# A spectral layer and two gated feed-forward layers: the first batch's inverse through memory, nine warming matmuls, shorter last stores

## The chip, the cores and the metric

The kernel runs on one NeuronCore of a Trainium2 chip. The metric is the device time of one execution in microseconds (us), the median of the runs shown.

## What is computed

`x` is 2 batches of 3008 rows by 256 columns, all in float32.

```python
X = np.fft.rfft(x, axis=1)                 # along the 3008 rows
Yr = Xr @ w_r - Xi @ w_i + b_r             # complex 256x256 mix
Yi = Xr @ w_i + Xi @ w_r + b_i
Y  = soft_threshold(Yr, 0.01) + 1j * soft_threshold(Yi, 0.01)
y  = np.fft.irfft(Y, n=3008, axis=1)       # 6016 rows by 256
y  = (sigmoid(y @ w_gate) * (y @ w_val)) @ w_out          # 256 -> 1536 -> 256
out = (silu(y @ w2_gate) * (y @ w2_val)) @ w2_out
```

## The kernel before, in words

**The transform.** 3008 is 47 times 64, and a row index splits into `(j, p)` with 94 values of `j` and 32 of `p`. A first transform over `j` is a matmul with a 94x96 table, a second one over the other index is a matmul with one 128x128 table for each of 24 frequency groups, two groups (`KP`) at a time. The inverse takes the same two steps backwards: 12 matmul steps with the table `i1c`, then 16 column pairs `c` with the table `f2s`. In between the data must change its layout.

**First batch** (`spectral_first`, L264 to L400, and `stage3` with `early` set). Its operands are plain float32, which TensorE takes in two passes; a profile counts each pass as one matmul. It starts with five matmuls on a zeroed bfloat16 tile (`warm`, L178 to L181, called at L299), whose result nobody reads. The first transform is L306: 9 tasks, 128 passes, with 94 rows of `x` as the stationary operand. It ends in SBUF (`zt`). For each of 12 steps `i` come four transposes (`turn`, L334), the second transform (`forward`, L242), the mix (L255, float32r operands, one pass each), the threshold and the inverse (L352). In the inverse the result `y` is stationary and the table moves, 128 columns at a time, so the result comes out with the channels on the partitions. ScalarE copies it into `zz` (L357), a tile that holds the whole batch. `stage3` then turns each column pair back by four transposes (L490), copies it to `z4` and multiplies by `f2s` (L501). The first `S3` = 6 pairs are done before the feed-forward loop begins (L636), the other 10 inside it, one for each unit.

**Second batch.** `spectral_second` does the same work inside the feed-forward loop, one piece per unit: `stage1` (16 column pairs, L219, three float32r matmuls each), `stage2` (12 steps) and `stage3`. Between its stages the data goes through two scratch tensors in memory, `scr1[1]` and `scr2[1]`: a store in one layout (L207, L454) and a load in the other (L408, L485). The first `E1` = 3 of its 16 column pairs are taken out of `stage1` and done ahead of the loop as one float32 matmul each (`fill`, L577); `filled` copies and stores them. Two of these matmuls stand beside the last inverse of the first batch, the third ahead of the loop.

**Feed-forward.** The rest, and most of the time, are units of 12 matmuls L636 and 6 matmuls L662 for each chunk of 512 rows and each of 12 weight blocks. VectorE and ScalarE decode the weights (`load_ff`) ahead of them.

**The end.** `turn_out` (L693 to L723) turns the last chunk of 384 rows and stores it to `out` by seven DMAs of 8, 94, 26, 68, 60, 34 and 94 rows of 1 KB, all on SP's queue.

**What sets the order.** Up to the feed-forward loop every engine follows the order in which the program is written. A DMA is issued by the engine that it is written for, in that engine's order: an SP instruction that waits holds what is behind it on SP.

Of the kernel before, what the change touches and what calls it, by code (L numbers as in the profile page):

```python
# [20 lines left out]
PP = 32  # L21
# [8 lines left out]
NA = 8  # L30
E1 = 3
S3 = 6
# [5 lines left out]
def tile_kernel(ctx, tc, x, w_r, w_i, b_r, b_i, wts, f1, f2, s2, i1, i1f, eye, one, out):  # L38
# [138 lines left out]

    def warm(n):  # L178
        for i in range(n):
            pw = ps_b.tile([P, 512], F32, tag="f", name=f"warm{i}")  # L180
            nc.tensor.matmul(pw, idle[:, 0:P], idle, start=True, stop=True)  # L181
# [81 lines left out]

    def spectral_first(zz, ps):  # L264
        NS = KH // KP
# [5 lines left out]
        with tc.tile_pool(name="z0", bufs=1, reuse_waits="tile") as z0:  # L271
# [8 lines left out]
            with tc.tile_pool(name="p1", bufs=1, reuse_waits="tile") as fp:  # L280
# [17 lines left out]
                nc.vector.memset(idle, 0.0)  # L298
                warm(5)  # L299
                next(tables)  # L300
# [26 lines left out]
            with tc.tile_pool(name="p2", bufs=1, reuse_waits="tile") as fp:  # L327
# [19 lines left out]
                def inverse(i, ks=range(KP)):  # L347
                    y, t = Y[i], table(i1c, i)
                    pi = bank(f"pi_0_{i}_{ks[0]}").rearrange("p (k d c) -> p k d c", k=KP, d=2)
                    for k in ks:  # L350
                        for d in range(2):
                            nc.tensor.matmul(pi[:, k, d, :], y[:, k, d * P:(d + 1) * P], t[:, k, :],  # L352
                                             start=True, stop=True)
                    k0, k1 = ks[0], ks[-1] + 1
                    dst = zz.rearrange("p d a (q k) -> p d (a q) k", q=4)
                    src = pi.rearrange("p k d c -> p d c k")
                    nc.scalar.copy(dst[:, :, :, KP * i + k0:KP * i + k1], src[:, :, :, k0:k1])  # L357

# [14 lines left out]
                for i in range(NS + 1):  # L373
                    if i + 1 < NS:
                        turn(i + 1)
                    if i < NS:
                        forward(i)
                    if i:
                        mix(i - 1, 0)
                    if 0 < i < last:  # L380
                        advance(dec, 1 + i % 2)
                    if i > last:
                        shrink(last, slice(0, 1))
                    if i > 1:
# [92 lines left out]

    def stage3(b, fp, ps, zz=None, direct=(), early=None):
        NS = PP // 2
        Z, V = {}, {}  # L480

        def load(c, ps):
            z4 = Z[c] = fp.tile([96, 2, 256], F32, tag="z4", bufs=4, name=f"z4_{b}_{c}")
            if zz is None:
                nc.sync.dma_start(z4, by_k1(scr2[b], slice(2 * c, 2 * c + 2)))  # L485
                return
            pt = ps.tile([P, 2, 256], F32, tag="f", name=f"p4_{b}_{c}")
            for q in range(2):
                for d in range(2):
                    nc.tensor.transpose(pt[:96, q, d * P:(d + 1) * P], zz[:, d, 2 * c + q, :], eyes)  # L490
            if early and c % 2:
                nc.vector.tensor_copy(z4, pt[:96])
            else:
                nc.scalar.copy(z4, pt[:96])

# [22 lines left out]

        c0 = 0
        if early:  # L520
# [9 lines left out]
        ps = ps[0] if early else ps  # L530
        ahead = 3 if zz is None else 1
        for c in range(c0 + len(Z), c0 + ahead):
            load(c, ps)
        for c in range(c0, NS):
            if c + ahead < NS:
                load(c + ahead, ps)
            inverse(c, ps)
            store(c)
            yield True

    def spectral_second(b, ps):
        with tc.tile_pool(name="fz", bufs=1, reuse_waits="tile") as fz:
            second = stage2(b, ps, fz)
            with tc.tile_pool(name="p1", bufs=1, reuse_waits="tile") as fp:
                for c, _ in enumerate(stage1(b, ps, fp, E1)):
                    if c == 5:
                        next(second)
                    yield True
# [3 lines left out]
        with tc.tile_pool(name="p3", bufs=2, reuse_waits="tile") as fp:  # L552
            yield from stage3(b, fp, ps)

# [7 lines left out]
    pz = pzs.enter_context(tc.tile_pool(name="pz", bufs=1, reuse_waits="tile", side="right"))  # L562
    zz = pz.tile([P, 2, PP, 96], F32, name="zz")
    f1f = pz.tile([NJ, P], F32, name="f1f")
# [4 lines left out]
    def load_fill(c):  # L569
        xb = x[1].rearrange("(j p) c -> j p c", p=PP)  # L570
        x1[c] = px.tile([NJ, 2, 256], F32, tag="x1", bufs=E1, name=f"x1_{c}")
        nc.sync.dma_start(x1[c][0:80], xb[0:80, 2 * c:2 * c + 2, :])
        nc.sync.dma_start(x1[c][80:94], xb[80:94, 2 * c:2 * c + 2, :])
# [5 lines left out]
    def filled(c, copy):  # L579
        z1 = px.tile([96, 2, 256], F32, tag="z1e", bufs=2, name=f"z1e_{c}")  # L580
        copy(z1, p1e.pop(c)[:96])
        nc.sync.dma_start(by_k1(scr1[1], slice(2 * c, 2 * c + 2)), z1)

    xs, late_ps = {}, []
    with tc.tile_pool(name="ps_b", bufs=8, space=PSUM) as ps_b:
        spectral_first(zz, ps_b)
        late_pools.append(ctx.enter_context(tc.tile_pool(name="wq", bufs=1, reuse_waits="tile")))
# [6 lines left out]
        def third_first():  # L594
            with tc.tile_pool(name="p3z", bufs=2, reuse_waits="tile") as fp:
                yield from stage3(0, fp, late_ps, zz, [split_x(0, c) for c in range(RC)], ps_b)
# [95 lines left out]
    def turn_out(ci, o):  # L692
# [9 lines left out]
        dst = out.rearrange("(b j p) c -> b p j c", b=B, p=PP)  # L702
        ob = mp.tile([P, 4, 256], F32, tag="ob", bufs=RC, name=f"ob{ci}")
        for j in range(0, tn, 256):
            pt = ps_f.tile([P, 2, 256], F32, tag="f", name=f"pt{ci}_{j}")
# [5 lines left out]
            for a, k in enumerate(js):  # L711
# [154 lines left out]
```

## Time and profile before

| what | value |
|---|---|
| median of 3 runs | 1378.81 us (1378.71 to 1380.22) |
| the profiled execution's own time | 1378.57 us |
| its span | 1376.5 us |
| TensorE busy (PE) | 1362.9 us, 99% of the span |
| VectorE busy (DVE) | 731.4 us, 53% |
| ScalarE busy (ACT) | 538.3 us, 39% |
| DMA, mean over the span | 55 GB/s |
| last matmul to the end of the span | 1366.85 to 1376.5 us |

Times in the profile are in us from the start of the span. The profile's chain that ended last lies on PE for 97% of the span, so what counts is how long PE takes from one matmul to the next. Matmuls overlap in the records: the time that one occupies is the distance from its start to the next start, not its length. PEclk is the TensorE clock that the profile shows as granted, as a share of full speed; GB/s is what the DMA engines moved.

### The profile page before, as it was taken

The numbers are of one execution on the slowest core, as the hardware profiler recorded it, in microseconds if no ns is written. First come the engines' busy times: TensorE is split into PE (matmuls) and PEld (weight loads), VectorE is DVE, ScalarE is ACT, GpSimd is POOL, SyncE is SP. The second block draws the span as 40 slices with busy tenths as digits, with TensorE's granted clock in tenths as the row PEclk, the third lists the DMA queues.
The fourth block names the chain that finished last, engine by engine and source line by source line (L and its number), as shares of the span: only waits on it lengthen the run. The fifth ranks groups of instructions, "written<-read, shape, count | busy, mean of one in ns | idle before, by whom it ended". The sixth has DMA issues, their size and how long they took to land.

```text
span 1376.5 us, 16890 instructions
## 1 busy us (share of the span) xinstructions
PE 1362.9 (99%) x6784; PEld 1163.2 (85%) x6784; DVE 731.4 (53%) x1110; ACT 538.3 (39%) x941; POOL 11.0 (1%) x26
## 2 busy tenths in 40 slices
PE   9999999999999999999999999999999999999997
PEld 8998888888888888888889988888888888888896
DVE  1558984555334865633344755555455555555553
ACT  1655554444334443433333433333333333333332
POOL 1000000000000000000000000000000000000000
PEclk9999999999999999999999999999999999999999
DMA  8222442333332320200002101001101101100000
GB/s 212 67 78 83 147 127 82 108 108 103 100 110 80 100 77 0 77 31 31 1 27 77 50 1 31 24 7 32 31 1 31 32 0 31 31 6 26 27 16 12
DMA packets 57202, 76.35 MB, mean 55 GB/s; under 512 B 6084, under 2 KB 40615, under 8 KB 57124
## 3 DMA queue, kind: packets, MB, share of 16 engines
q1 hardware_dynamic: 54980, 71.69, 17.0%
q0 software_dynamic: 2144, 3.58, 1.3%
q8 instruction: 53, 0.87, 0.3%
q14 instruction: 25, 0.20, 0.0%
HBM read 51.53 MB, written 23.72 MB: 55 GB/s over the span
## 4 chain that ended last, share of the span: by engine, by line
PE 97%; DMA 1%; DVE 1%; ACT 0%; SPq 0%; issue 0%; ACTq 0%
PE pg L636 56%; PE po L662 28%; PE pm L255 5%; PE p L501 2%; PE p L306 2%; PE p L242 1%; PE pi L352 1%; PE pt L710 1%; PE p L219 1%; PE pi L448 1%; PE p L490 1%; PE pt L334 0%; DMA xr<-in_x_dram 0%; DMA xin<-xT 0%; PE p1e L577 0%; DVE yl L440 0%
## 5 line engine op out<-in xcount | busy, mean ns | idle before, releaser
L636 PE MATMUL pg<-fxh,wh 128*128 128x512 f32 (+1 forms) x1152 | 446.1, 387 | 0.0
L636 PE MATMUL pg<-fxl,wh 128*128 128x512 f32 (+1 forms) x1152 | 443.5, 385 | 0.0
L636 PE MATMUL pg<-fxh,wl 128*128 128x512 f32 (+1 forms) x1152 | 443.4, 385 | 0.0
L640 ACT ACTIVATE sg<-pg 128x512 f32<-128x512 f32 (+1 forms) x288 | 169.6, 589 | 362.2 <-PE pg L636 361.6
L644 DVE TENSOR_TENSOR h<-sg,pg 128x512 f32<-128x512 f32 (+1 forms) x288 | 194.5, 675 | 188.8 <-ACT sg L640 183.7
L647 ACT CAST hh<-h 128x512 fp32r<-128x512 f32 (+1 forms) x288 | 176.6, 613 | 300.2 <-DVE h L644 299.2
L649 DVE TENSOR_TENSOR hl<-h,hh 128x512 fp32r<-128x512 f32 (+1 forms) x288 | 195.9, 680 | 154.7 <-ACT hh L647 152.3
L636 PEld LDWEIGHTS pg<-fxh,wl 128*128 128x128 f32 x1152 | 216.2, 188 | 41.4
L636 PEld LDWEIGHTS pg<-fxh,wh 128*128 128x128 f32 x1152 | 216.5, 188 | 41.0 <-DVE fxl L512 0.2
L636 PEld LDWEIGHTS pg<-fxl,wh 128*128 128x128 f32 x1152 | 216.4, 188 | 39.9 <-issue 0.2
L662 PE MATMUL po<-hh,wh 128*128 128x512 f32 (+1 forms) x576 | 223.6, 388 | 0.3 <-ACT hh L647 0.3
L662 PE MATMUL po<-hh,wl 128*128 128x512 f32 (+1 forms) x576 | 221.9, 385 | 0.0
L662 PE MATMUL po<-hl,wh 128*128 128x512 f32 (+1 forms) x576 | 221.6, 385 | 0.0
L642 DVE TENSOR_TENSOR sg<-sg,pg 128x512 f32<-128x512 f32 (+1 forms) x144 | 97.4, 676 | 157.9 <-ACT sg L640 157.7
L662 PEld LDWEIGHTS po<-hh,wl 128*128 128x128 f32 x576 | 108.1, 188 | 20.8
L662 PEld LDWEIGHTS po<-hh,wh 128*128 128x128 f32 x576 | 108.2, 188 | 20.5 <-ACT hh L647 0.6
L662 PEld LDWEIGHTS po<-hl,wh 128*128 128x128 f32 x576 | 108.2, 188 | 20.2 <-DVE hl L649 0.2
L255 PE MATMUL pm<-wmh,Xh 128*128 128x256 f32 x192 | 54.2, 282 | 0.9 <-DVE Xl L234 0.9
L255 PE MATMUL pm<-wmh,Xl 128*128 128x256 f32 x192 | 53.7, 280 | 0.0
L255 PE MATMUL pm<-wml,Xh 128*128 128x256 f32 x192 | 53.7, 280 | 0.0
L625 DVE TENSOR_TENSOR fxl<-xin,fxh 128x512 fp32r<-128x512 f32 (+1 forms) x44 | 28.5, 677 | 19.4 <-ACT fxh L624 19.2
L255 PEld LDWEIGHTS pm<-wmh,Xh 128*128 128x128 f32 x192 | 36.2, 188 | 3.1 <-DVE Xl L234 2.7
(103 smaller groups left out, 854.2 us busy)
## 6 DMA issues: line engine op xcount, KB each, us to landing
raw<-in_moe_w_gate_dram SPq DMA_DIRECT2D x24, 256.0 KB
raw<-in_moe_w_val_dram SPq DMA_DIRECT2D x24, 256.0 KB
raw<-in_moe_w_out_dram SPq DMA_DIRECT2D x24, 256.0 KB
xin<-x2T SPq DMA_DIRECT2D x11, 512.0 KB
xT<-xo SPq DMA_DIRECT2D x26, 188.0 KB
x2T<-xo SPq DMA_DIRECT2D x9, 512.0 KB
xin<-xT SPq DMA_DIRECT2D x8, 512.0 KB
i1s<-in_tab_i_dram POOLq DMA_DIRECT2D x12, 256.0 KB, 4.2
```

The costliest lines, as they stand in the source:

```text
L219: nc.tensor.matmul(pt[c][:96], f1s[:, w, :], v, start=(i == 0), stop=(i == 2))
L255: nc.tensor.matmul(pm[:, k, :], a, w, start=(j == 0), stop=(j == len(ops) - 1))
L306: nc.tensor.matmul(pt[:, a], xt[:, a, d * P:(d + 1) * P], f1f, start=True, stop=True)
L501: nc.tensor.matmul(pt[:, d, q * NJ:(q + 1) * NJ], z[:, q, d * P:(d + 1) * P], f2s, start=True, stop=True)
L625: nc.vector.tensor_tensor(xl[:, k, :tn], xin[:, k, :tn], xh[:, k, :tn], op=ALU.subtract)
L636: nc.tensor.matmul(pg[:, s, :tn], w[:, 2 * s + k, :], v[:, k, :tn], start=(i == 0), stop=(i == 5))
L640: nc.scalar.activation(sg[:, :tn], pg[:, 0, :tn], AF.Sigmoid)
L642: nc.vector.tensor_tensor(sg[:, :tn], sg[:, :tn], pg[:, 0, :tn], op=ALU.mult)
L644: nc.vector.tensor_tensor(h[:, :tn], sg[:, :tn], pg[:, 1, :tn], op=ALU.mult)
L647: nc.scalar.copy(hh[:, :tn], h[:, :tn])
L649: nc.vector.tensor_tensor(hl[:, :tn], h[:, :tn], hh[:, :tn], op=ALU.subtract)
L662: nc.tensor.matmul(o[d][:, :tn], w[:, 4 + d, :], v[:, :tn], start=(first and d not in [q for q, _, _ in ops[:i]]), stop=(last and d not in ...
```

## The change

The first batch's inverse now holds the table still and moves `y`, 256 columns at a time, so a result comes out in the layout that the second batch has. It is copied to a small tile `z3` and stored to `scr2[0]`; `stage3` loads it back in the other layout, seven column pairs (`Z4`) ahead. `zz` and the transposes L490 are gone. `E1` goes from 3 to 8: eight column pairs of the second batch are done as fills, seven of them between the last inverse and the first L501, with their copies on VectorE and ScalarE in turn and their stores on POOL's queue. `warm` runs nine matmuls in place of five. The last chunk's stores are cut to at most 80 rows; three of the now nine (34, 60 and 14 rows) are issued by ScalarE.

```diff
-E1 = 3
+E1 = 8
+Z4 = 7
...
-    def warm(n):
+    def warm(n, banks):
         for i in range(n):
-            pw = ps_b.tile([P, 512], F32, tag="f", name=f"warm{i}")
+            if i < banks:
+                pw = ps_b.tile([P, 512], F32, tag="f", name=f"warm{i}")
             nc.tensor.matmul(pw, idle[:, 0:P], idle, start=True, stop=True)
...
-                warm(5)
+                warm(9, 7)
...
                 def inverse(i, ks=range(KP)):
                     y, t = Y[i], table(i1c, i)
-                    pi = bank(f"pi_0_{i}_{ks[0]}").rearrange("p (k d c) -> p k d c", k=KP, d=2)
+                    k0, k1 = ks[0], ks[-1] + 1
+                    pi = bank(f"pi_0_{i}_{k0}").rearrange("p (k c) -> p k c", k=KP)
                     for k in ks:
-                        for d in range(2):
-                            nc.tensor.matmul(pi[:, k, d, :], y[:, k, d * P:(d + 1) * P], t[:, k, :],
-                                             start=True, stop=True)
-                    k0, k1 = ks[0], ks[-1] + 1
-                    dst = zz.rearrange("p d a (q k) -> p d (a q) k", q=4)
-                    src = pi.rearrange("p k d c -> p d c k")
-                    nc.scalar.copy(dst[:, :, :, KP * i + k0:KP * i + k1], src[:, :, :, k0:k1])
+                        nc.tensor.matmul(pi[:, k], t[:, k, :], y[:, k, :], start=True, stop=True)
+                    z3 = fp.tile([P, KP, 256], F32, tag="z3", bufs=2, name=f"z3_0_{i}_{k0}")
+                    nc.scalar.copy(z3[:, k0:k1], pi[:, k0:k1])
+                    nc.sync.dma_start(by_p(scr2[0], slice(KP * i + k0, KP * i + k1)), z3[:, k0:k1])
...
-                    if 7 < i < 8 + E1:
-                        load_fill(i - 8)
+                    if 1 < i < 2 + E1:
+                        load_fill(i - 2)
                 inverse(last, (0,))
                 fill(0)
                 inverse(last, (1,))
-                fill(1)
-                filled(0, nc.vector.tensor_copy)
-                filled(1, nc.vector.tensor_copy)
...
-        def load(c, ps):
-            z4 = Z[c] = fp.tile([96, 2, 256], F32, tag="z4", bufs=4, name=f"z4_{b}_{c}")
-            if zz is None:
-                nc.sync.dma_start(z4, by_k1(scr2[b], slice(2 * c, 2 * c + 2)))
-                return
-            pt = ps.tile([P, 2, 256], F32, tag="f", name=f"p4_{b}_{c}")
-            for q in range(2):
-                for d in range(2):
-                    nc.tensor.transpose(pt[:96, q, d * P:(d + 1) * P], zz[:, d, 2 * c + q, :], eyes)
...
+        def load(c):
+            Z[c] = zp.tile([96, 2, 256], F32, tag="z4", bufs=bufs, name=f"z4_{b}_{c}")
+            nc.sync.dma_start(Z[c], by_k1(scr2[b], slice(2 * c, 2 * c + 2)))
...
         if early:
-            for c in range(4):
-                load(c, early)
+            for c in range(bufs):
+                load(c)
+            yield True
             for c in range(S3):
                 inverse(c, early)
                 store(c)
-                if 4 + c <= S3:
-                    load(4 + c, early)
-            c0 = S3
+            c0, ahead = S3, bufs - 1
+            for c in range(bufs, c0 + ahead):
+                load(c)
...
     def filled(c, copy):
-        z1 = px.tile([96, 2, 256], F32, tag="z1e", bufs=2, name=f"z1e_{c}")
+        z1 = pz.tile([96, 2, 256], F32, tag="z1e", bufs=4, name=f"z1e_{c}")
         copy(z1, p1e.pop(c)[:96])
-        nc.sync.dma_start(by_k1(scr1[1], slice(2 * c, 2 * c + 2)), z1)
+        nc.gpsimd.dma_start(by_k1(scr1[1], slice(2 * c, 2 * c + 2)), z1)
...
         third = third_first()
         next(third)
-        fill(2)
-        filled(2, nc.vector.tensor_copy)
+        filled(0, nc.vector.tensor_copy)
+        for c in range(1, E1):
+            fill(c)
+            filled(c, nc.scalar.copy if c % 2 else nc.vector.tensor_copy)
+        next(third)
...
-                    step = min(n - r, NJ - jj)
-                    nc.sync.dma_start(dst[pcol // PP, pcol % PP, jj:jj + step, :], ob[r:r + step, k // 128, :])
+                    step = min(n - r, NJ - jj, 80 if end else NJ)
+                    late.append((dst[pcol // PP, pcol % PP, jj:jj + step, :], ob[r:r + step, k // 128, :]))
+                    if not end or k == 0 or step > 60:
+                        nc.sync.dma_start(*late.pop())
                     r += step
+            if j + 256 >= tn:
+                for pair in late:
+                    nc.scalar.dma_start(*pair)
```

**TensorE at the seam, before.** These are PE's instructions from the first batch's last inverse (`pi`) to its column pairs (`p`); `p1e` is a fill.

```order
L352 MATMUL pi_11_1_1026<-i1c_687,y_11_983 128x128 x2
L577 MATMUL p1e_1030<-x_1_872,f1f 128x512
L490 MATMUL p_0_0_1054<-eyes,zz 96x128 x4
L490 MATMUL p_0_1_1061<-eyes,zz 96x128 x4
L490 MATMUL p_0_2_1068<-eyes,zz 96x128 x4
L490 MATMUL p_0_3_1075<-eyes,zz 96x128 x4
L501 MATMUL p_0_0_1081<-f2s,z_0_0_1053 128x94 x4
L490 MATMUL p_0_4_1089<-eyes,zz 96x128 x4
L501 MATMUL p_0_1_1095<-f2s,z_0_1_1060 128x94 x4
```

The transposes read `zz` and stand ahead of each column pair.

The same place in the changed kernel, whose line numbers are its own (L354 is the inverse, L564 the fill, L488 the column pair):

```order
L354 MATMUL pi_11_1_1047<-y_11_1003,i1c_704 128x256
L564 MATMUL p1e_1084<-x_1_512,f1f 128x512
L564 MATMUL p1e_1089<-x_2_574,f1f 128x512
L564 MATMUL p1e_1094<-x_3_638,f1f 128x512
L564 MATMUL p1e_1099<-x_4_706,f1f 128x512
L564 MATMUL p1e_1104<-x_5_767,f1f 128x512
L564 MATMUL p1e_1109<-x_6_830,f1f 128x512
L564 MATMUL p1e_1114<-x_7_895,f1f 128x512
L488 MATMUL p_0_0_1119<-f2s,z_0_0_1067 128x94 x4
L488 MATMUL p_0_1_1126<-f2s,z_0_1_1069 128x94 x4
```

Seven fills now stand where the first transposes stood, and the column pairs follow one on another.

**SP's queue at the seam, changed.** `scr_0` is `scr2[0]`, `z_0_11_0` and `z_0_11_1` are the last two `z3` tiles, the other `z` are `z4` tiles. Before the change SP issued nothing for these.

```order
L357 DMA scr_0_78<-z_0_10_0_1022 128x512
L357 DMA scr_0_78<-z_0_11_0_1042 128x256
L357 DMA scr_0_78<-z_0_11_1_1049 128x256
L481 DMA z_0_0_1067<-scr_0_78 96x2x256
L481 DMA z_0_1_1069<-scr_0_78 96x2x256
L481 DMA z_0_2_1071<-scr_0_78 96x2x256
L481 DMA z_0_3_1073<-scr_0_78 96x2x256
L481 DMA z_0_4_1075<-scr_0_78 96x2x256
```

Every load of `z4` reads from all 12 stores, so the first one waits on SP until the last store has landed.

## Rows read from the trace of the kernel before

**Rows 1.** The page: the chain that ended last, by engine.

```profile
PE 97%; DMA 1%; DVE 1%; ACT 0%; SPq 0%; issue 0%; ACTq 0%
```

**Rows 2.** Timeline of PE, 0 to 45 us: start, length, instruction, passes, [idle before <-releaser].

```profile
1.19 2.31 PE L181 MATMUL warm<-idle 128*128 128x512 bf16 x5 [1.19 <-DVE idle L298]
4.22 3.75 PE L306 MATMUL p<-f1f,xr 94*128 94x128 f32 x16 [0.71 <-DMA f1f<-in_tab_f_dram]
8.28 24.23 PE L306 MATMUL p<-f1f,xr 94*128 94x128 f32 x112 [0.31 <-DMA xr<-in_x_dram]
32.31 0.42 PE L334 MATMUL pt<-eyes,zt 128*128 128x128 f32 x1
...
34.50 1.67 PE L242 MATMUL p<-s2c,z 128*128 128x128 f32 x8
36.01 0.60 PE L334 MATMUL pt<-eyes,zt 128*128 128x128 f32 x4
36.44 1.06 PE L242 MATMUL p<-s2c,z 128*128 128x128 f32 x8
37.26 0.36 PE L255 MATMUL pm<-bmov,ones 128*128 128x256 f32 x1
```

**Rows 3.** Windows of the start: length, busy time by engine, PEclk, DMA share, GB/s.

```profile
0.00:17.40 17.40, 15.18 (x64) 13.22 (x65) 2.10 (x5) 3.29 (x7) 4.47 (x14) 1.00 0.93 202
17.40:20.40 3.00, 3.00 (x16) 3.00 (x16) 0.56 (x1) 0.27 (x1) 0.00 (x0) 1.00 1.05 281
```

**Rows 4.** Windows, the stretch in which DVE makes the mix tables (same columns).

```profile
29.60:35.12 5.52, 5.33 (x25) 4.70 (x25) 2.95 (x8) 1.79 (x4) 0.00 (x0) 1.00 0.07 26
```

**Rows 5.** Timeline of PE, 97 to 110 us, the seam to the feed-forward loop.

```profile
97.50 1.02 PE L577 MATMUL p1e<-x,f1f 94*128 94x512 f32 x2
98.36 0.61 PE L352 MATMUL pi<-i1c,y 128*128 128x128 f32 x4
98.80 1.02 PE L577 MATMUL p1e<-x,f1f 94*128 94x512 f32 x2
99.85 1.95 PE L490 MATMUL p<-eyes,zz 128*96 128x128 f32 x16
...
102.51 0.60 PE L490 MATMUL p<-eyes,zz 128*96 128x128 f32 x4
102.95 1.03 PE L501 MATMUL p<-f2s,z 96*128 96x94 f32 x8
103.81 0.60 PE L490 MATMUL p<-eyes,zz 128*96 128x128 f32 x4
...
108.69 0.80 PE L636 MATMUL pg<-fxh,wh 128*128 128x512 f32 x1
```

**Rows 6.** Timeline of PE, 183 to 193 us: a column pair of the second batch's first stage.

```profile
186.98 0.63 PE L219 MATMUL p<-xh,f1s 94*96 94x512 f32 x2
...
187.68 0.40 PE L636 MATMUL pg<-fxh,wh 128*128 128x512 f32 x1
```

**Rows 7.** Timeline of all engines, 352 to 363 us: SP at the second batch's seam.

```profile
353.28 0.33 SPq L454 DMA_DIRECT2D scr<-z  x1
...
355.48 1.80 SPq L485 DMA_DIRECT2D z<-scr  x4
```

**Rows 8.** Windows, 356.5 to 359.8 us, while those four loads land.

```profile
356.50:359.80 3.30, 3.30 (x20) 2.78 (x19) 0.69 (x1) 0.74 (x2) 0.00 (x0) 1.00 0.73 233
```

**Rows 9.** Timeline, 1355 to 1377 us: the last matmuls and the last stores on SP.

```profile
1365.81 1.04 PE L710 MATMUL pt<-eyes,ot 128*128 128x128 f32 x6 [0.18 <-ACT ot L699]
...
1367.17 2.39 SPq L721 DMA_DIRECT2D out_dram<-ob  x7
```

**Rows 10.** Windows of the end, 1370.0 to 1375.5 us.

```profile
1370.00:1370.50 0.50, 0.00 (x0) 0.00 (x0) 0.00 (x0) 0.00 (x0) 0.00 (x0) 0.71 0.50 92
...
1371.50:1372.00 0.50, 0.00 (x0) 0.00 (x0) 0.00 (x0) 0.00 (x0) 0.00 (x0) 0.50 0.14 49
...
1375.00:1375.50 0.50, 0.00 (x0) 0.00 (x0) 0.00 (x0) 0.00 (x0) 0.00 (x0) 0.50 0.00 0
```

More of the change, by code (lines that the diff above doesn't have):

```diff
@@ L260, in shrink_of, with spectral_first @@
         nc.vector.scalar_tensor_tensor(out=y, in0=pm, scalar=LAM, in1=y, op0=ALU.add, op1=ALU.min)
-    def spectral_first(zz, ps):
+    def spectral_first(ps):
         NS = KH // KP
@@ L474, in stage2, with stage3 @@
             yield True
-    def stage3(b, fp, ps, zz=None, direct=(), early=None):
+    def stage3(b, fp, ps, zp, bufs, direct=(), early=None):
         NS = PP // 2
         Z, V = {}, {}
-        def load(c, ps):
-            z4 = Z[c] = fp.tile([96, 2, 256], F32, tag="z4", bufs=4, name=f"z4_{b}_{c}")
-            if zz is None:
-                nc.sync.dma_start(z4, by_k1(scr2[b], slice(2 * c, 2 * c + 2)))
-                return
-            pt = ps.tile([P, 2, 256], F32, tag="f", name=f"p4_{b}_{c}")
-            for q in range(2):
-                for d in range(2):
-                    nc.tensor.transpose(pt[:96, q, d * P:(d + 1) * P], zz[:, d, 2 * c + q, :], eyes)
[L491 to L494, printed above, removed]
+        def load(c):
+            Z[c] = zp.tile([96, 2, 256], F32, tag="z4", bufs=bufs, name=f"z4_{b}_{c}")
+            nc.sync.dma_start(Z[c], by_k1(scr2[b], slice(2 * c, 2 * c + 2)))
         def inverse(c, ps):
@@ L519, in stage3 @@
         c0 = 0
+        ahead = 3
         if early:
-            for c in range(4):
-                load(c, early)
+            for c in range(bufs):
+                load(c)
+            yield True
             for c in range(S3):
@@ L525, in stage3 @@
                 store(c)
-                if 4 + c <= S3:
-                    load(4 + c, early)
-            c0 = S3
+            c0, ahead = S3, bufs - 1
+            for c in range(bufs, c0 + ahead):
+                load(c)
             yield True
-        ps = ps[0] if early else ps
-        ahead = 3 if zz is None else 1
+            ps = ps[0]
         for c in range(c0 + len(Z), c0 + ahead):
-            load(c, ps)
+            load(c)
         for c in range(c0, NS):
             if c + ahead < NS:
-                load(c + ahead, ps)
+                load(c + ahead)
             inverse(c, ps)
@@ L545, in spectral_second @@
                 for c, _ in enumerate(stage1(b, ps, fp, E1)):
-                    if c == 5:
+                    if c == 4:
                         next(second)
@@ L552, in spectral_second @@
         with tc.tile_pool(name="p3", bufs=2, reuse_waits="tile") as fp:
-            yield from stage3(b, fp, ps)
+            yield from stage3(b, fp, ps, fp, 4)
     late_pools = []
@@ L562, in tile_kernel @@
     pz = pzs.enter_context(tc.tile_pool(name="pz", bufs=1, reuse_waits="tile", side="right"))
-    zz = pz.tile([P, 2, PP, 96], F32, name="zz")
     f1f = pz.tile([NJ, P], F32, name="f1f")
@@ L570, in load_fill @@
         xb = x[1].rearrange("(j p) c -> j p c", p=PP)
-        x1[c] = px.tile([NJ, 2, 256], F32, tag="x1", bufs=E1, name=f"x1_{c}")
+        x1[c] = (pz if c < E1 else px).tile([NJ, 2, 256], F32, tag="x1", bufs=E1 if c < E1 else 2, name=f"x1_{c}")
         nc.sync.dma_start(x1[c][0:80], xb[0:80, 2 * c:2 * c + 2, :])
@@ L579, in filled @@
     def filled(c, copy):
-        z1 = px.tile([96, 2, 256], F32, tag="z1e", bufs=2, name=f"z1e_{c}")
+        z1 = pz.tile([96, 2, 256], F32, tag="z1e", bufs=4, name=f"z1e_{c}")
         copy(z1, p1e.pop(c)[:96])
-        nc.sync.dma_start(by_k1(scr1[1], slice(2 * c, 2 * c + 2)), z1)
+        nc.gpsimd.dma_start(by_k1(scr1[1], slice(2 * c, 2 * c + 2)), z1)
     xs, late_ps = {}, []
     with tc.tile_pool(name="ps_b", bufs=8, space=PSUM) as ps_b:
-        spectral_first(zz, ps_b)
+        spectral_first(ps_b)
         late_pools.append(ctx.enter_context(tc.tile_pool(name="wq", bufs=1, reuse_waits="tile")))
@@ L595, in third_first @@
             with tc.tile_pool(name="p3z", bufs=2, reuse_waits="tile") as fp:
-                yield from stage3(0, fp, late_ps, zz, [split_x(0, c) for c in range(RC)], ps_b)
+                yield from stage3(0, fp, late_ps, pz, Z4, [split_x(0, c) for c in range(RC)], ps_b)
             pzs.close()
@@ L703, in turn_out @@
         ob = mp.tile([P, 4, 256], F32, tag="ob", bufs=RC, name=f"ob{ci}")
+        late = []
         for j in range(0, tn, 256):
```

## The prediction, made before the changed kernel ran

> **What bounds the kernel now.** I read the chain that ended last first. It lies on PE for 97% [rows 1], so a part of the change counts by what it does to PE's distances from start to start, and outside PE only the end counts, where PE is done at 1365.81 + 1.04 = 1366.85 us [rows 9] and the stores run on to 1376.5. Then I read PE's timeline at the start. There the reader should see one thing that the clock column doesn't show: that column says 1.00 from the first window on [rows 3], but 112 passes L306 take 32.31 - 8.28 = 24.03 us, 0.215 us each, while 8 passes L242 of the same 128 columns take 37.26 - 36.44 = 0.82 us later, 0.103 each [rows 2]. That is a factor of two, the clock's two levels, 1.2 and 2.4 GHz: the whole first transform ran at the lower one. The rise lies inside the L242 group at 34.50, whose 8 passes take 36.01 - 34.50 = 1.51 us; 6.1 of them slow and 1.9 fast give that, so it rose at about 35.8. Then the seam between the first batch and the feed-forward loop [rows 5], the same seam of the second batch, which already goes through memory [rows 7, 8], and the end [rows 9, 10].
>
> **The change, part by part.**
>
> *Transposes L490.* All 16 groups of four go. One takes 102.95 - 102.51 = 0.44 us of PE [rows 5]. 16 x 0.44 = -7.0 us. Their copies leave ACT and DVE too, which is worth nothing by itself: PE doesn't wait for them in the loop.
>
> *Inverse L352.* Eight passes of 128 columns per step become four of 256. Columns streamed are the same: 0. Bounds -0.5 and +0.6 over 12 steps, from 0.44 us for four passes of 128 [98.36 to 98.80 in rows 5] against 0.43 for one pass of 512 (97.50 to 98.36 is two). ACT copies `z3` where it copied `zz`. The 13 stores on SP wait for ACT there, and weight and table loads queue behind them; PE needs none of these within the step, so 0.
>
> *Fills.* Five more of them, 98.36 - 97.50 = 0.86 us each [rows 5]: +4.3. Five column pairs leave `stage1`, 187.68 - 186.98 = 0.70 us each [rows 6]: -3.5. Net +0.8. PE's wait between the fill at 98.80 (over at 99.66) and the first L490 at 99.85 goes: -0.2.
>
> *The seam.* This is the new wait. The first `z4` load must wait until the last `z3` store has landed, and the first L501 for that load. What covers it is seven fills, 7 x 0.86 = 6.0 us from 98.80: PE comes to L501 at 104.8 on the old time scale. The second batch's seam shows the price: store issued at 353.28, first load at 355.48, 2.2 us later [rows 7]. Four loads of 192 KB (786 KB) land from about 356.5 to 359.8 at 233 GB/s [rows 8], so the first lands some 2 us after its issue and each further one about 0.8 us later. The last inverse ends by 98.80, its copy by about 99.4, so: store 99.5, load 101.7, landed about 103.7, 1 us ahead of need. The later loads come every 0.8 us and L501 wants them every 0.86 (102.95 to 103.81), but the eight fill stores, 1.5 MB, share the DMA engines, which at the worst doubles the pace: five loads x 0.8 = 4 us late. Bounds 0 and +4, less the 1 us of lead; I take +1, nearer to the free case, since the stores are spread out by the fills' own pace. SP stands still in that wait; behind it are `xT` stores and weight loads that nobody needs for some 10 us.
>
> *Nine warming matmuls.* Five take 0.43 us each, from 1.19 [rows 2]; nine end at 1.19 + 9 x 0.43 = 5.05, and L306 started at 4.22. If nothing else comes of it, that costs 0.8, of which the 0.31 us wait at 8.28 gives back a part: +0.5. If the clock rises by them, L306 runs at 0.103 us a pass, its 112 passes in 11.5 us, and then no longer PE but the data set the pace. By 17.40 us the trace moved 202 GB/s x 17.4 = 3.51 MB [rows 3]; that is `x[0]` (3.08 MB) and POOL's constants (0.43 MB). The next 3.0 us bring 0.84 MB: `eyes`, the first table and `wraw` (0.85 MB). SP issues in the same order after the change and the DMA engines are full already (share 0.93 and 1.05), so these times stay. PE's last task then ends at 17.4 + 16 x 0.103 = 19.0, and 3.3 to 5.0 us of transposes and L242 follow (32.31 to 37.26 was 4.95, part of it slow): the mix at 22.3 to 24.0. The mix also needs its tables, 2.95 us of DVE work [rows 4] behind `wraw` at 20.4: 23.4 at the earliest. I take 24.0 against 37.26: -13.2. Next late is the second table, behind 1.9 MB of weights, at about 20.4 + 7.5 = 27.9, just when it is wanted; ends -10 and -14.
>
> Does the clock rise? For: this trace saw it rise 3.5 us after L306 gave way to other float32 work; nine dense matmuls are 3.84 us of work no thinner than that, five were 2.1 us and did nothing. Against: those 3.5 us stood behind 24 us of L306, the nine stand behind an idle engine. And would it stay? From 97.50 to 108.69 PE did float32 passes on 94 and 96 rows at full rate [rows 5], and at the end the clock fell only in the window from 1370.0 [rows 10], 3 us after PE stopped. The gaps for data at the start are below 2 us. So it would stay. The Trainium skill (TensorE: Matmul & The Clock Gate, "Part 1: The HAM clock gate") says that the half clock is the default, that sustained activity releases it, and that the moment differs from run to run because the monitor isn't started by the kernel. By that rule the new kernel's runs could fall into two groups, at the forecast and at rival A. The three runs of before lie within 1.5 us, which neither bears that out nor excludes it.
>
> *The last stores.* SP issues seven, the last by 1369.56 [rows 9], yet data flow until 1375.0 and the span ends 1.5 us later. From 1371.5 on the DMA share is 0.14 [rows 10], 2 of 16 engines: the 94-row piece uses few. The kernel's loads of `x` go in 80 and 14 rows and keep the share at 0.93 and above [rows 3]. With all pieces at such shares, data end 1 to 1.5 us after the last issue: about 1371, -4.6 at best. The 34- and 68-row pieces may stay narrow: -2 at least. I take -4.1. The Trainium skill (DMA: Bandwidth & Descriptors, "Why a DMA increments its semaphore by 16 and not by 1") says that a DMA takes the largest number of engines up to 16 that divides its rows: 2 for 94 rows, as the share shows, 16 for 80, 14 for 14, but 2 for 34 and 4 for 68. By that rule the two busiest engines carry 53 rows in place of 135, and the estimate is the same, -4.
>
> **Sum.** -7.0 + 0.8 - 0.2 + 1.0 - 13.2 - 4.1 = -22.7 us on the profiled execution's 1378.57 us, which lies 0.24 below the median: **1356 us**. Its own range, with the ends of each term, is 1350 to 1361.
>
> **Rivals.**
> - *A: the clock doesn't rise in the start.* -22.7 + 13.2 + 0.5 = -9.0: 1369.7 us. For it: 24 us of L306 without a gap didn't raise it. Against it: the rise at 35.8. Chance 0.29.
> - *B: the end stays as it is*, because the narrow pieces or ScalarE's issues set it: 1360 us. For it: 34 and 68 rows remain whole. Chance 0.06.
> - *C, slower: the round trip outlasts its cover and the clock falls.* If the first `z4` lands later than 104.8 + 3.4 = 108.2 us, PE has been idle for as long as it was at the end before the clock fell there. Then 48 passes L501 take 0.107 us more each, 5.1 us, and the first feed-forward unit (2.8 us) twice its time: 3.4 + 5.1 + 2.8 = 11.3, 10.3 more than in the sum. On top of A that is 1380 us, above today; on top of the forecast, 1366. It decides when the trip from the last inverse takes 9.4 us where the second batch's takes about 5. For it: fill stores on the same engines at the same time. Chance 0.05 on top of A.
>
> **How the numbers follow.** Forecast 0.60, A 0.29, B 0.06, C 0.05. 80% needs the forecast's range and A, with a little for A's own ends: 1350 to 1371 us. Faster by more than 0.2%, which is 2.8 us and about what a measurement of this kernel tells from no change: the forecast, A and B, 0.95. Within it 0.02, slower 0.03, both out of C.
>
> **What would show it.** Passes L306 0.1 us apart from about 5 to 9 us on and gaps for `xr` between the tasks; the mix starting near 24 us. No transposes in the seam, L501 right behind the last fill with waits below 1 us for `z4`. Stores over by about 1371 on a span some 4 us shorter behind the last matmul. Wrong: L306 still 0.215 us apart (A), a wait of over 3 us ahead of the first L501 and slow passes behind it (C), or a DMA share of 0.14 for several us at the end (B).

## The result and the profile after

| what | before | after |
|---|---|---|
| median | 1379.28 us (8 executions, 1378.27 to 1380.22) | 1363.61 us (8 executions, 1361.46 to 1374.55) |
| ratio, 95% interval | | 0.9895 (0.9876 to 0.9913) |
| profiled execution, its span | 1378.57, 1376.5 us | 1365.84, 1363.7 us |
| mix starts | 37.26 us | 26.00 us |
| first matmul of the feed-forward loop starts | 108.69 us | 103.32 us |
| last matmul to the end of the span | 9.65 us | 5.83 us |

The change is worth 15.7 us, where 22.7 were forecast. The granted clock of an execution, a mean over its span, goes with its time: 0.997 in the three shortest of the eight (1361.46 to 1362.46 us), 0.994 in the profiled one, 0.987 in the longest. So the profiled execution, 2.2 us above the median, had the low clock for longer than most. Of the runs further down, the profiled execution of *before_nine_warm* took 2280.78 us at a granted clock of 0.556 and stands in no comparison.

The chain on the page still lies on PE, with a little more DMA in it than before [rows 1]:

```profile
PE 97%; DMA 2%; ACT 1%; SPq 0%; issue 0%; DVE 0%; ACTq 0%
```

PE's timeline at the start, to be laid beside [rows 2] (L308, L336, L244 and L257 are what L306, L334, L242 and L255 were):

```profile
1.19 4.02 PE L183 MATMUL warm<-idle 128*128 128x512 bf16 x9 [1.19 <-DVE idle L300]
5.01 2.04 PE L308 MATMUL p<-f1f,xr 94*128 94x128 f32 x16
8.20 2.02 PE L308 MATMUL p<-f1f,xr 94*128 94x128 f32 x16 [1.16 <-DMA xr<-in_x_dram]
10.58 3.92 PE L308 MATMUL p<-f1f,xr 94*128 94x128 f32 x32 [0.36 <-DMA xr<-in_x_dram]
14.74 7.38 PE L308 MATMUL p<-f1f,xr 94*128 94x128 f32 x64 [0.23 <-DMA xr<-in_x_dram]
21.95 0.27 PE L336 MATMUL pt<-eyes,zt 128*128 128x128 f32 x1
...
26.00 0.37 PE L257 MATMUL pm<-bmov,ones 128*128 128x256 f32 x1
```

From 5 us on a pass takes 0.113 us ((21.95 - 14.74) / 64) where it took 0.215: the clock is at 2.4 GHz from the first passes on. PE waits for rows three times, 1.75 us in all, and not again from 14.74 us to the end of the first transform: the data are ahead of it. The mix starts 11.26 us earlier than before.

PE at the seam, from behind the last inverse (L564 is the fill, L488 the column pair, L626 the first feed-forward matmul; of before [rows 5]):

```profile
87.25 6.17 PE L564 MATMUL p1e<-x,f1f 94*128 94x512 f32 x14
93.26 1.92 PE L488 MATMUL p<-f2s,z 96*128 96x94 f32 x16
96.90 6.71 PE L488 MATMUL p<-f2s,z 96*128 96x94 f32 x32 [1.72 <-DMA z<-scr]
103.32 0.77 PE L626 MATMUL pg<-fxh,wh 128*128 128x512 f32 x1
103.89 0.63 PE L626 MATMUL pg<-fxl,wh 128*128 128x512 f32 x1
104.32 0.63 PE L626 MATMUL pg<-fxh,wl 128*128 128x512 f32 x1
```

The same stretch in windows (columns as in [rows 3]), and what SP issued:

```profile
96.00:97.00 1.00, 0.10 (x1) 0.13 (x2) 0.29 (x1) 0.38 (x1) 0.42 (x1) 1.00 1.05 385
97.00:98.00 1.00, 1.00 (x7) 1.00 (x8) 0.40 (x1) 0.94 (x3) 0.73 (x2) 0.67 0.85 282
98.00:103.00 5.00, 5.00 (x26) 5.00 (x25) 2.41 (x6) 1.58 (x4) 1.25 (x3) 0.50 0.61 185
103.00:107.00 4.00, 4.00 (x12) 3.23 (x12) 0.33 (x1) 0.63 (x2) 0.00 (x0) 0.50 0.15 35
107.00:108.00 1.00, 1.00 (x5) 0.82 (x4) 0.00 (x0) 0.00 (x0) 0.00 (x0) 0.71 0.96 238
108.00:112.00 4.00, 4.00 (x25) 3.48 (x24) 3.00 (x5) 1.63 (x4) 0.00 (x0) 1.00 1.04 231
```

```profile
80.47 7.74 SPq L357 DMA_DIRECT2D scr<-z  x4
89.65 4.47 SPq L481 DMA_DIRECT2D z<-scr  x7
```

The transposes are gone and the first two column pairs (16 passes) stand right behind the fills. The third waits 1.72 us for its load, while the DMA engines are full (share 1.05, 385 GB/s). Then the granted clock falls to 0.50 and stays there until 107 us: 32 passes take 0.20 us each instead of 0.11, and the first nine feed-forward matmuls are 0.42 us apart or more instead of 0.23. From the fills' start to L626 PE needs 16.07 us.

The end, of the timeline and in windows ([rows 9, 10] are before's):

```profile
1356.83 1.04 PE L701 MATMUL pt<-eyes,ot 128*128 128x128 f32 x6 [0.18 <-ACT ot L689]
...
1358.19 2.27 SPq L714 DMA_DIRECT2D out_dram<-ob  x6
...
1358.47 1.82 ACTq L718 DMA_DIRECT2D out_dram<-ob  x3
```

```profile
1361.00:1362.00 1.00, 0.00 (x0) 0.00 (x0) 0.00 (x0) 0.00 (x0) 0.00 (x0) 0.50 0.43 135
1362.00:1363.00 1.00, 0.00 (x0) 0.00 (x0) 0.00 (x0) 0.00 (x0) 0.00 (x0) 0.50 0.00 0
```

In the last microsecond with data the share is 0.43, where before it lay at 0.14, and nothing flows after 1362.

PE's longest waits, of the view of waits (us in total, times, longest):

```profile
PE pm L257 <- ACT z L450: 2.1, 1, 2.1
PE p L308 <- DMA xr<-in_x_dram: 1.7, 3, 1.2
PE p L488 <- DMA z<-scr: 1.7, 1, 1.7
```

The first lies in the second batch's mix, behind a feed-forward input whose load SP issued at 257.65 and for which ScalarE waited until 263.67. Before, PE waited 0.91 us there. Behind this wait the clock fell a second time, as PE's timeline shows:

```profile
267.80 0.42 PE L257 MATMUL pm<-wmh,Xh 128*128 128x256 f32 x1 [2.12 <-ACT z L450]
268.02 0.41 PE L257 MATMUL pm<-wmh,Xl 128*128 128x256 f32 x1
...
271.43 0.29 PE L257 MATMUL pm<-wml,Xh 128*128 128x256 f32 x1
271.55 0.28 PE L257 MATMUL pm<-wmh,Xh 128*128 128x256 f32 x1
```

Up to 271.2 us the matmuls are 0.21 us apart, behind it 0.12, and the granted clock is 0.50 from 268 to 271. The 24 matmuls take 4.45 us here and 2.91 in *seam_filled_wait*, where the clock held behind a wait of 1.75 us at the same place. So the second fall cost the profiled execution 1.5 us.

### The profile page after: what moved, and what is told of

The parts are those of the page before. It is cut to its first block, busy times and chain, and to the rows that moved or that the text cites. A ratio compares the mean times of both kernels' runs of the same rounds, so it can differ in the third digit from the quotient of the medians.

```text
span 1363.7 us, 16708 instructions
## 1 busy us (share of the span) xinstructions
PE 1350.0 (99%) x6671; PEld 1147.4 (84%) x6671; DVE 723.4 (53%) x1098; ACT 528.0 (39%) x927; POOL 16.1 (1%) x34
## 4 chain that ended last, share of the span: by engine, by line
PE 97%; DMA 2%; ACT 1%; SPq 0%; issue 0%; DVE 0%; ACTq 0%
PE pg L626 56%; PE po L652 28%; PE pm L257 5%; PE p L488 2%; PE p L244 2%; PE pi L354 1%; PE pt L701 1%; DMA xr<-in_x_dram 1%; PE p L308 1%; PE pi L445 1%; DMA z<-scr 0%; DMA xin<-xT 0%; PE p L221 0%; PE pt L336 0%; SPq L290 0%
## 5 line engine op out<-in xcount | busy, mean ns | idle before, releaser
L626 PE MATMUL pg<-fxh,wh 128*128 128x512 f32 (+1 forms) x1152 | 446.6, 388 | 0.0
L626 PE MATMUL pg<-fxh,wl 128*128 128x512 f32 (+1 forms) x1152 | 444.0, 385 | 0.0
L626 PE MATMUL pg<-fxl,wh 128*128 128x512 f32 (+1 forms) x1152 | 444.0, 385 | 0.0
L626 PEld LDWEIGHTS pg<-fxh,wl 128*128 128x128 f32 x1152 | 216.7, 188 | 41.4
L626 PEld LDWEIGHTS pg<-fxh,wh 128*128 128x128 f32 x1152 | 216.9, 188 | 40.4
L626 PEld LDWEIGHTS pg<-fxl,wh 128*128 128x128 f32 x1152 | 216.9, 188 | 40.0
L257 PE MATMUL pm<-wmh,Xh 128*128 128x256 f32 x192 | 54.9, 286 | 2.1 <-ACT z L450 2.1
L257 PE MATMUL pm<-wmh,Xl 128*128 128x256 f32 x192 | 54.5, 284 | 0.0
L257 PE MATMUL pm<-wml,Xh 128*128 128x256 f32 x192 | 54.4, 283 | 0.0
L257 PEld LDWEIGHTS pm<-wmh,Xh 128*128 128x128 f32 x192 | 36.9, 192 | 4.5 <-ACT z L450 2.9
```

Of the source, the lines that this page charges most:

```text
L257: nc.tensor.matmul(pm[:, k, :], a, w, start=(j == 0), stop=(j == len(ops) - 1))
L626: nc.tensor.matmul(pg[:, s, :tn], w[:, 2 * s + k, :], v[:, k, :tn], start=(i == 0), stop=(i == 5))
```

## The experiments

Theory T, from the trace of the changed kernel: the parts do what the prediction said, but the 1.7 us wait in the seam lets the clock fall, and that takes back most of what the seam should give. The kernel before, run beside the experiments, had medians of 1379.64 to 1380.07 us.

**One part alone, or one undone**

*before_nine_warm*: the kernel before with `warm(9, 7)`, nothing else.

> The kernel before with nine warming matmuls in place of five, nothing else. Theory T (the nine lift the clock to 2.4 GHz by about 5 us, and it stays): the passes of the first transform come 0.11 us apart, the mix starts at 26 us instead of 37.3, and the time falls by about 11 us to 1368, with some runs that lose part of it again. Rival R1 (the rise at 5 us in the changed kernel comes from something else in it): passes stay 0.215 us apart and the time is that of before plus 0.5, about 1380.

Measured: 1369.71, 1369.74 and 1368.25 us, ratio 0.9921 (0.9904 to 0.9937). The nine matmuls alone are worth 9.9 us, which excludes R1's 1380. When the clock rose in these three no trace shows; in the changed kernel's the same matmuls raise it by 5 us.

*after_five_warm*: the changed kernel without that part.

```diff
-                warm(9, 7)
+                warm(5, 5)
```

> The changed kernel with five warming matmuls as before. T: the first transform runs at 0.215 us a pass again, the mix starts at 37 us, the time is about 11 us above the changed kernel, 1375, and the seam still waits some 1.7 us for its loads and falls to 1.2 GHz there. R1: no difference to the changed kernel, 1363.6.

Measured: 1374.18 us, ratio 0.9957 (0.9940 to 0.9974). PE's timeline shows the slow start of before (128 passes in 27.7 us):

```profile
4.22 27.95 PE L308 MATMUL p<-f1f,xr 94*128 94x128 f32 x128 [0.72 <-DMA f1f<-in_tab_f_dram]
31.96 0.42 PE L336 MATMUL pt<-eyes,zt 128*128 128x128 f32 x1
```

Its third pair waited 1.79 us, and the clock fell there as in the changed kernel (32 passes in 115.13 - 108.31 = 6.82 us):

```profile
108.31 7.11 PE L488 MATMUL p<-f2s,z 96*128 96x94 f32 x32 [1.79 <-DMA z<-scr]
```

So the fall in the seam doesn't need the early start.

*before_short_stores*: the kernel before with the cut of the last stores alone.

```diff
-                    step = min(n - r, NJ - jj)
-                    nc.sync.dma_start(dst[pcol // PP, pcol % PP, jj:jj + step, :], ob[r:r + step, k // 128, :])
+                    step = min(n - r, NJ - jj, 80 if end else NJ)
+                    late.append((dst[pcol // PP, pcol % PP, jj:jj + step, :], ob[r:r + step, k // 128, :]))
+                    if not end or k == 0 or step > 60:
+                        nc.sync.dma_start(*late.pop())
...
+                for pair in late:
+                    nc.scalar.dma_start(*pair)
```

> The kernel before with the last chunk's stores cut to at most 80 rows as in the change, nothing else. The end after the last matmul should shrink from 9.65 us to 5.8 us, as it did in the changed kernel, and the time by 3.8 us to 1375.5. If the cut is worth nothing by itself and the shorter end comes from something earlier, 1379.3.

Measured: 1375.72 us, ratio 0.9969 (0.9956 to 0.9981), -3.9 us. The last matmul ends at 1366.76 + 1.04 and the span at 1373.4, 5.6 us later. What is left for the seam part is the difference to *after_five_warm*, 1374.18 - 1375.72 = -1.5 us (with two intervals of about 2 us each, so its sign is open). The three parts add up: -9.9 - 3.9 - 1.5 = -15.3, against -15.7 together. By the ratios they are -10.9, -4.3 and -1.6, -16.8 against -14.5, so the agreement is good to 2 us or so.

**What costs in the seam**

*stores_behind_loads*: the fill results are copied back over the tile they came from, and SP stores them behind the seven loads, so these stores no longer share the DMA engines with the loads. (The input tiles get 96 rows for it, in lines that aren't shown.)

```diff
...
-        z1 = pz.tile([96, 2, 256], F32, tag="z1e", bufs=4, name=f"z1e_{c}")
+        z1 = x1.pop(c)
         copy(z1, p1e.pop(c)[:96])
-        nc.gpsimd.dma_start(by_k1(scr1[1], slice(2 * c, 2 * c + 2)), z1)
+        nc.sync.dma_start(by_k1(scr1[1], slice(2 * c, 2 * c + 2)), z1)
```

> The changed kernel with the eight fill results copied back over their own input tiles and stored by SP behind the seven z4 loads, so that the loads have the DMA engines to themselves. T (in the seam the loads are late because the fill stores share the engines, and the wait of 1.7 us lets the clock fall): no wait ahead of the third column pair, no fall of the clock, passes at 0.11 us and the first feed-forward unit at full rate: 1.7 + 3 + 2 us less, about 1357. Rival R2 (the thin float32 work of the seam lets the clock fall whether it waits or not): the wait goes, but the passes still slow to 0.2 us: about 1361.5.

Measured: 1358.86, 1359.02, 1359.64 and, profiled, 1368.57 us; ratio 0.9865 (0.9833 to 0.9897). PE's timeline at the seam:

```profile
97.87 6.17 PE L564 MATMUL p1e<-x,f1f 94*128 94x512 f32 x14
103.88 5.49 PE L488 MATMUL p<-f2s,z 96*128 96x94 f32 x48
109.16 0.48 PE L626 MATMUL pg<-fxh,wh 128*128 128x512 f32 x1
```

The same 14 and 48 passes take 11.29 us and not 16.07, with no wait and 0.11 us a pass, so the thin float32 passes ("thin" for the 94 and 96 rows that they use) don't lower the clock by themselves here. The seam is mended; what made this one execution long is at the start, below. The three others lie about 2 us above T's 1357.

*seam_filled_wait*: the changed kernel, its stores and loads as they are, with work put into the wait.

```diff
             for c in range(S3):
+                if c == 2:
+                    warm(8, 1)
                 inverse(c, early)
```

> The changed kernel with eight dense warming matmuls ahead of the third column pair of the seam, where the matrix engine waits 1.7 us for that pair's load; the stores and loads stay as they are, so the data come no earlier. Theory T (the wait let the clock fall, and the clock, not the wait, is most of the seam's cost): eight matmuls at 2.4 GHz take about 1.7 us, just the wait; the third and fourth pair's passes then take 0.11 us each instead of 0.21 (32 x 0.1 = 3.2 us less) and the first feed-forward unit runs at full rate (about 2 us less): 4.5 to 5 us less than the changed kernel's 1363.6, some 1358.5 to 1359.5, and the granted clock stays 1.00 from 97 to 108 us. Rival R (the thin float32 passes of the fills and pairs themselves lower the clock, with or without the wait): passes of 0.2 us as before, 1363 to 1365. Rival R' (the slow passes come from the transfers, which load the memory ports at 375 GB/s): the same time as R, though the granted clock shows 1.00.

Measured: 1359.35 us (1358.63 to 1360.96), ratio 0.9852 (0.9840 to 0.9865). PE's timeline (its L628 is the changed kernel's L626), and the windows in which the DMA engines are as full as before:

```profile
93.61 1.92 PE L488 MATMUL p<-f2s,z 96*128 96x94 f32 x16
95.37 1.89 PE L183 MATMUL warm<-idle 128*128 128x512 bf16 x8
97.13 3.78 PE L488 MATMUL p<-f2s,z 96*128 96x94 f32 x32
100.69 0.48 PE L628 MATMUL pg<-fxh,wh 128*128 128x512 f32 x1
```

```profile
96.00:97.00 1.00, 1.00 (x6) 0.39 (x4) 0.36 (x1) 0.16 (x1) 0.35 (x1) 1.00 1.06 374
97.00:98.00 1.00, 1.00 (x10) 0.90 (x9) 0.17 (x1) 1.00 (x3) 0.58 (x2) 1.00 1.00 366
```

Nothing comes earlier here; PE is only kept busy for 1.76 us. The 32 passes take 3.56 us instead of 6.42, the feed-forward starts at full rate, and the median is 4.3 us lower. This separates the two costs in the profiled executions: the wait itself is 1.7 us, the clock that falls behind it some 5. Traffic at 366 GB/s slows no pass. One thing stays open: the dummy matmuls fill 1.76 us that *stores_behind_loads* doesn't spend, yet the medians of the two are equal. Where that version loses it no trace shows, since its only trace is of the long execution.

*five_warm_seam_filled*: the same eight matmuls in the kernel with five warming ones.

> The kernel with five warming matmuls (1374.2 us; it has the change's seam and its short stores) and eight dense matmuls ahead of the third column pair of the seam. Against the kernel before with the short stores alone (1375.7 us) it then differs by the seam part alone, without the fall of the clock. Theory T (the seam part is what the prediction summed, about 5.4 us less, and the clock gave 4 us of it back): 1369 to 1371 us, the third and fourth pair at 0.11 us a pass, the mix still starting near 37 us. Rival (the seam part is worth only the 1.5 us that the two kernels without the matmuls differ by, and the gain of the filled wait belongs to the early clock): 1372.5 to 1374.5.

Measured: 1371.10 us (1369.01 to 1371.62), ratio 0.9937 (0.9922 to 0.9952); T's range missed by 0.1 us, the rival's by 1.4. Against *before_short_stores* the seam part is worth -4.6 us once the clock holds (-5.4 by the prediction's terms, and -4.6 by them if the 1.76 us that the eight matmuls take stand in place of its +1), and -1.5 where it falls.

**The start: why some executions are longer**

One of the changed kernel's eight executions took 1374.55 us at a granted clock of 0.987 (the others 0.994 to 0.997). In *stores_behind_loads* the profiled execution is such a one, timeline and windows:

```profile
4.61 1.95 PE L308 MATMUL p<-f1f,xr 94*128 94x128 f32 x16
8.65 2.02 PE L308 MATMUL p<-f1f,xr 94*128 94x128 f32 x16 [2.09 <-DMA xr<-in_x_dram]
11.13 20.82 PE L308 MATMUL p<-f1f,xr 94*128 94x128 f32 x96 [0.46 <-DMA xr<-in_x_dram]
```

```profile
8.00:10.00 2.00, 1.35 (x12) 1.38 (x13) 0.00 (x0) 0.19 (x1) 0.00 (x0) 1.00 1.00 252
10.00:12.00 2.00, 1.54 (x10) 1.38 (x10) 0.56 (x1) 0.29 (x1) 0.00 (x0) 0.75 1.45 258
12.00:20.00 8.00, 8.00 (x39) 8.00 (x39) 1.12 (x2) 0.96 (x2) 0.00 (x0) 0.50 1.13 245
```

The clock had risen (16 passes in 1.95 us) and held through 16 more passes behind a wait of 2.09 us for rows of `x`. It fell at about 11.0 us (0.75 is the mean of two levels over 10 to 12), in a second wait of 0.46 us, and stayed low through 96 thin passes without a gap; the mix started at 36.62. Which of the two waits took it, or whether both did, this trace doesn't tell. Three kernels on top of *stores_behind_loads* vary the start.

*stores_behind_loads_7_warm*: `warm(7, 7)`.

> The same with seven warming matmuls instead of nine (five left the clock at 1.2 GHz until 37 us, nine raised it by 5 us). If the rise comes with the amount of dense work, seven are a case between: either each execution is like nine (1358.5 to 1360) or like five (about 1370), and a mixture says that the moment of the look differs between executions. Theory T expects a mixture or all slow; a rival by which only the last matmul's end against the data's arrival counts (seven end 0.9 us earlier, so the waits for data are as long or longer) expects all slow, near 1370.

Measured: 1367.93 us (1367.26 to 1368.27), ratio 0.9912 (0.9900 to 0.9925): all four long, which T and its rival both expected, so that the times don't tell them apart. The trace does more: the clock rose here too, and fell in the wait (timeline, windows):

```profile
4.15 2.30 PE L308 MATMUL p<-f1f,xr 94*128 94x128 f32 x16
8.37 24.24 PE L308 MATMUL p<-f1f,xr 94*128 94x128 f32 x112 [1.92 <-DMA xr<-in_x_dram]
```

```profile
6.00:8.00 2.00, 0.46 (x5) 0.26 (x3) 0.36 (x1) 0.32 (x1) 0.52 (x1) 1.00 0.92 180
8.00:10.00 2.00, 1.63 (x8) 1.66 (x8) 0.00 (x0) 0.00 (x0) 0.00 (x0) 0.54 0.91 235
```

*stores_behind_loads_16_warm*: `warm(16, 7)`.

> The kernel with the fill results stored behind the loads, with sixteen warming matmuls instead of nine at the start. Seven more at about 0.215 us are 1.5 us, which moves the first task's passes from 5.0 to about 6.5 us and takes the waits for the second and third task's data (0.4 to 2.1 us) away. Theory T (the clock sometimes falls in those data waits and then stays low through the thin float32 passes until about 36 us, which is what the executions of 1368 to 1375 us are): every execution between 1358 and 1360.5, none above 1362. Rival (the thin passes let the clock fall at a moment of chance, with no wait needed): executions of 1368 and more remain. Rival (the added matmuls simply delay the start): all executions up by 1 to 1.5 us, about 1360.5.

Measured: five executions from 1357.69 to 1360.06 us and one of 1368.94 (clock 0.990); ratio 0.9861 (0.9840 to 0.9882). T missed: it expected none above 1362. The profiled execution kept its clock, but the wait had only moved: 1.24 us ahead of the passes at 15.89. Where the long one lost its clock no trace shows, so the rival by which the thin passes lose it without a wait isn't excluded.

*stores_behind_loads_guarded*: nine at the start, and dense matmuls where PE waits for rows.

```diff
                     if t + 6 < len(tasks):
                         load(t + 6)
+                    if t in (1, 2, 4):
+                        warm({1: 6, 2: 2, 4: 1}[t], 1)
```

> The same with nine warming matmuls at the start and six, two and one further ones behind the first, second and fourth group of passes, where the matrix engine waits for the next rows (about 1.2, 0.4 and 0.2 us). Theory T: waits are filled, the clock stays at 2.4 GHz, every execution between 1358.5 and 1360. Rival (the clock falls by chance in thin passes): executions of 1368 and more remain. Against sixteen in front: equal, or up to 1 us dearer if the nine together end late.

Measured: 1360.63 us (1358.72 to 1362.94), ratio 0.9862 (0.9848 to 0.9876), clock 0.999 or 1.000 in all four, but three of them above T's 1360. The start of its timeline:

```profile
5.00 2.68 PE L308 MATMUL p<-f1f,xr 94*128 94x128 f32 x16
7.52 1.46 PE L183 MATMUL warm<-idle 128*128 128x512 bf16 x6
```

The first 16 passes take 2.52 us where 16 x 0.113 = 1.81 are 2.4 GHz's: here the clock rose some passes later than in the changed kernel.

*seam_filled_start_guarded*: the changed kernel with this guard and the eight matmuls in the seam.

> The changed kernel with both fillings: nine dense matmuls at the start and six, two and one behind the first, second and fourth group of passes, and eight ahead of the third column pair of the seam. Theory T: the waits in which the clock fell are filled, so the clock shows 0.999 or more in every execution and none lies more than 3 us above the lowest; the added matmuls move the mix from 26.0 to about 27.2 us, so the median is 1359 to 1361, no better than with the seam alone filled (1359.4). Rival (the clock falls now and then for a reason other than these waits): an execution of 1368 or more among the six.

Measured: 1360.26 us (1359.92 to 1360.78, four executions), ratio 0.9861 (0.9844 to 0.9877), clock 0.999 in all. The mix starts at 26.04 us, not at the 27.2 that T had put. The guarded starts had no long execution in eight, the other versions of the change with nine or sixteen matmuls three in 22. At that rate eight in a row without one come by chance in about a third of cases ((19/22) to the eighth is 0.31), so that the guard removes them isn't shown. That the clock can fall in a wait in this stretch the two traces above show.

By the median the best versions are *seam_filled_wait* and *stores_behind_loads*, both about 1359.3 us, 4.3 below the change and 20 below the kernel before. The guarded medians lie about 1 us higher, which the intervals don't tell apart.

## Why the prediction was right, and where it was off

- **Nine warming matmuls, -13.2 (ends -10 and -14): right in mechanism, 2 to 3 us too large.** In the trace the mix starts 11.26 us earlier, where 24.0 against 37.26 is 13.26, and alone the part gives 9.9 (8.7 to 13.2 by its interval). The mis-sized step is "PE's last task then ends at 17.4 + 16 x 0.103 = 19.0", which lets the data set the pace to the end. A pass took 0.113 us, the waits at the beginning cost 1.75, and from 14.74 us PE worked off what had landed: 21.95. The sentence behind it, that the gaps "are below 2 us. So it would stay", fits seven of eight executions. The eighth, 1374.55 us at a clock of 0.987, has no trace; the nearest that has one (*stores_behind_loads*, 0.990) lost the clock in such gaps, so by that the eighth would have come close to rival A's start on another road: not a clock that doesn't rise, but one that is lost again.
- **The clock's rise.** Behind nine dense matmuls the passes run at 2.4 GHz, where the clock stayed low through 24 us of thin passes [rows 2]. The Trainium skill (TensorE: Matmul & The Clock Gate, "Part 1: The HAM clock gate") has the moment of the rise differ from run to run. The traces agree: the same nine matmuls are over at 4.61 us in *stores_behind_loads* and at 5.0 in the changed kernel, and in *stores_behind_loads_guarded* some passes behind them still run slow. But what parts the long executions from the others isn't that moment as far as is traced: the two traces of the long group show an early rise and a fall in a wait for data.
- **The seam, +1 (bounds 0 and +4): the step that failed.** The round trip was well foreseen: the first load at 89.65 us where 101.7 - 11.55 = 90.15 was worked out (11.55 is how much earlier the last inverse starts, 98.36 against 86.81), the first pairs on time, a later one late by 1.7 us, because the fill stores share the DMA engines (each load waits for 13 stores, since the last step's go in two halves, and not for 12). But the sum held only the lateness. Beside the 11.29 us of the stretch without a wait it cost 1.72 of waiting, 6.42 - 3.56 = 2.9 of slow passes and 10 x 0.2 = 2 in the feed-forward: 6.6 us in the profiled execution, and on the median the 4.3 us that filling or removing the wait gave back. Rival C had this mechanism, put behind 3.4 us of idling, "as long as it was at the end before the clock fell there". In the seam half of that did. The rival should have stood on the forecast with a larger chance, as a fall behind a wait of 1 to 2 us.
- **Transposes -7.0, fills net +0.8, wait gone -0.2, inverse 0.** Together with a seam of +1 they make -5.4; -4.6 was measured where the clock holds, which the intervals don't tell apart. They were not tried one by one. In the trace nine groups of transposes and five column pairs are gone from the loops. No term had the second batch's wait for the late feed-forward input: in the profiled execution it took back 2.1 - 0.9 = 1.2 us and the fall behind it 1.5. How much of that is the change's own is open. The same wait is 1.20 us in *before_short_stores*, whose second batch is untouched, and 1.2 to 1.8 in the other changed versions, with no fall. The change also starts the second batch's `stage2` one column pair earlier (`c == 4` for `c == 5` in the loop over `stage1`, a line that the diff above doesn't show), which was not tried by itself.
- **The last stores, -4.1 (ends -2 and -4.6): right.** -3.9 alone, 9.65 - 5.83 = -3.8 in the trace. Data end 1.5 us after the last issue, as put. That the share in the last microsecond rises only to 0.43, and not to the 0.93 of the loads of `x`, agrees with the Trainium skill's rule (DMA: Bandwidth & Descriptors, "Why a DMA increments its semaphore by 16 and not by 1") that pieces of 34 and 68 rows use few engines; it did no harm, and rival B fell.
- **The sum.** -22.7 forecast, -15.7 measured: 3.3 of the 7.0 missing from the start, 3.9 from the seam (-5.4 against -1.5), 0.2 from the end, 0.4 the other way between single parts and the whole.
- **The range.** The forecast's own range was 1350 to 1361, and the median, 1363.61, lies above it. It lies inside the stated 1350 to 1371 because that was drawn out for rival A (whose own sum gives 1378.57 - 9.0 = 1369.6, not 1369.7), and A didn't come true. That the range held is luck in this; two terms were missed the same way, the start by 2 to 3 us and the seam by about 4.

## What to carry to other kernels

A wait of PE is priced by the wait and, where the clock falls behind it, by the clock: here 1.7 us of waiting cost 6.6 in the profiled execution. Where a wait stands ahead of thin passes, either order the queues so that what PE needs next doesn't share the DMA engines with stores nobody waits for, or put dense dummy matmuls into the wait; both gave the same 4.3 us on the median. A warm-up that ends before the data flow steadily can be lost again in the first wait for them.

## What the runs showed of the hardware that was not expected

- The clock fell in or behind waits of 1.72 us (changed kernel, seam), 1.79 (*after_five_warm*, seam), 1.92 (*stores_behind_loads_7_warm*, start) and 2.12 (changed kernel, second batch), and in the start of *stores_behind_loads* behind 2.09 and 0.46 together. It held in profiled executions behind 1.82 (*seam_filled_wait*, start), 1.75 (the same, second batch), 1.24 and 1.16. The length alone doesn't tell: 1.72 took it in one place and 1.82 left it in another.
- Low in the second batch's mix, it was back by 271.4 us, behind 16 of the mix's 128x256 matmuls (changed kernel).
- Low in the start, it stayed low through 24 us of gapless thin float32 passes (*stores_behind_loads_7_warm*, 8.37 to 32.4), yet such passes at 2.4 GHz kept it high (*stores_behind_loads*, 48 of them behind 14 fills).
- The granted clock shows 1.00 in windows whose passes run at 1.2 GHz, as long as it hasn't risen [rows 2, 3]; after a rise and a fall it shows 0.50. *before_short_stores*, whose passes run at 1.2 GHz for its first 35 us, lists 0.999; *stores_behind_loads_7_warm*, whose clock fell at 8 us and was low as long, lists 0.989.
